# Heads grouped by parity in a fused attention and feed-forward kernel: state products and scores in 64x32 tiles, weight sums continued in one bank, a new order

## The chip, the core and the metric

The kernel runs on one core of a Trainium2 chip. The metric is the device time of one execution in microseconds (us), as the median of several runs. A core has five engines with instruction queues of their own: TensorE (PE, with PEld for its weight loads), VectorE (DVE), ScalarE (ACT), GpSimd (POOL) and SyncE (SP, which here issues most DMAs). Each works through its queue in order and waits on semaphores. TensorE writes to PSUM, eight banks of 512 f32 columns on 128 partitions; the other operands lie in SBUF.

## What is computed

```python
# x [8, 8, 512, 64], state [8, 8, 32, 64]: batch, head, rows, D
scores = scale * x @ state^T                 # softmax over the 32 state rows
xread = softmax(scores) @ state
scores2 = scale * state @ x^T                # softmax over the 512 positions
sread = softmax(scores2) @ x
a = concat([xread, sread], rows)             # 544 rows a batch, heads side by side: 512 features
xn = (a - mean) / sqrt(var + 1e-6) * g_ln
out = a + relu(xn @ w_ch1) @ w_ch2           # w_ch1 [512, 2048], w_ch2 [2048, 512]
```

The weights arrive as 64-bit floats. f32 accuracy is kept by writing each f32 operand as a high and a low f16 half and summing the products high x high, high x low and low x high (`TERMS`).

## The kernel before, in words

*Units.* The 2,048 hidden features are cut into four units of 512 (u = 0 to 3). Because xread is a softmax times the state, xread @ w_ch1 is computed as softmax @ (state @ w_ch1): `state_products` (L660) makes for each batch and unit a `matrix` of 2 x 128 rows (8 heads x 32 state rows) by 512 features, and the products with the softmax numerators `ea` follow in `first_products` (L701, batch 0) and `products` (L799, batches 1 to 7). The second layer is a plain product in batch 0 (L715) and a Strassen form with seven products in batches 1 to 7 and for the 256 state rows at the end (L855, L808). It needs sums and differences of blocks of w2, made once a unit in `sums_of_weights` (L741): products with plus and minus the identity (`signs`), 256 columns each, into parts of two accumulator banks, 16 a unit and half, each difference then split into halves by ACT and DVE.

*Heads.* Heads are paired as g = h // 4, j = h % 4. The state halves `sh` are laid out twice over, so that `sT` [128, g, a, 128] holds, for each head, 64 rows and 64 rows once more; the other operand holds the high half of a head in one half of its 128 partitions and the low half in the other. One product over all 128 rows then gives two of the terms. In the state products (L665) and the scores (L403) a head is a tile of 128 rows x 32 columns; j picks the columns, g the call: eight products of 512 columns (two a, four j) a call. For this, w1's halves are first written to the buffers `raw` or `sums` and then copied by four DMAs a unit into `w1c` (L621), high beside low. The end needs w1's high halves whole, which eight more copies gather in `high` (L891).

*State read.* `read_state` (L475) multiplies, for each head and each of four chunks, the stacked halves of x (128 columns) with both halves of the transposed numerators (64 columns): 32 products (L479). The two 64-row parts of the result are then added by four f32 products with `fold`, two stacked identities (L492), recorded as eight passes.

*PSUM.* `accumulator` is a pool of four banks, `half` of two, `banks` one buffer of two banks. In batches 1 to 7, `banks` is claimed for the maxima, the scores, the state read and twice for mixing (L515); the state products use `half`, which the hidden blocks (L799) also use.

*Order.* The work is written as 175 streams of steps. `PLAN` (L40) lists all steps in one order, as stream:steps, and `issue` (L189) issues them so. Since each engine works in order, this list is each engine's order. Stream 0 is the gain, 1 the attention of batch 0, 2 to 5 the first-layer weights of units 0 to 3, 6 the state products of batch 0, 7 `first_products`, 8 to 11 the second-layer weights, 13 to 16 the second products of batch 0, 17 and 18 attention and state products of batch 1, 19 to 22 the weight sums. All DVE, ACT and POOL work is recorded under L186, the helper that issues a step.

*Weights of a unit* (`weights1`, L581): two loads, 64-bit words to f32 (ACT, DVE), means by four f32 products (L599), four DVE subtractions, sizes (ACT, L608), scale, high half (ACT) and low half (DVE).

Of the kernel before, what the change touches and what calls it, by code (L numbers as in the profile page):

```python
# [1 line left out]

# [6 lines left out]
F32 = mybir.dt.float32  # L9
# [179 lines left out]
def issue(tc, streams, plan):  # L189

    streams = [list(s) for s in streams]
    with tc.manual_schedule():
        for item in plan.split() or [f"{k}:0-{len(s)}" for k, s in enumerate(streams)]:
            k, n = item.split(":")
            n = [int(v) for v in n.split("-")]
            for f in streams[int(k)][n[0]:n[-1] + 1]:
                f()


@with_exitstack  # L200
def moe_attention(ctx: ExitStack, tc: tile.TileContext, x, state, g_ln, w1, w2, out):

    nc = tc.nc
# [24 lines left out]
    def rows(name):  # L233
        return block(8, "rows", 2, name)
# [744 lines left out]
```

## Time and profile before

| | |
|---|---|
| median of 3 runs | 667.59 us (666.89 to 668.29) |
| span of the profiled execution | 665.9 us |
| PE, DVE, ACT, POOL busy | 626.3, 498.0, 388.2, 216.7 us |
| chain that ended last | PE 90%, DVE 5%, DMA 2% |

The profiled execution is told by its span, from the first instruction to the last; the median of the runs is the device's time of whole executions, 1.7 us more. In the profile a group is line, engine, operation, output <- inputs, shape and count. "128*32" is a tile of 128 rows and 32 columns of TensorE. [...] "Chain" is the work followed back from the last instruction, at each step to what released it.

### The profile page before, as it was taken

What the parts mean: (1) busy time and instruction counts of PE and PEld (TensorE: products, weight loads), DVE (VectorE), ACT (ScalarE), POOL (GpSimd) and SP (SyncE); (2) the same over time, 40 slices, a digit from 0 to 9 for tenths busy, and PEclk for the clock granted to TensorE, in tenths of its full rate; (3) what the DMA queues carried; (4) which work ended last, traced back from release to release, by engine and by line L of the source; (5) the groups of instructions that cost most, each with busy time, mean ns of one, the idle gap of its engine ahead of it and who ended that gap; (6) DMA issues with size and microseconds to landing.
All of it is one profiled execution on the core that took longest, in us unless ns stands there. A gap on an engine that the chain in (4) does not pass through costs nothing.

```text
span 665.9 us, 14680 instructions
## 1 busy us (share of the span) xinstructions
PE 626.3 (94%) x5948; PEld 493.1 (74%) x5948; DVE 498.0 (75%) x1002; ACT 388.2 (58%) x699; POOL 216.7 (33%) x189
## 2 busy tenths in 40 slices
PE   0676999999999999999999999999999999999996
PEld 0242755548887887788888888878778887888885
DVE  5989986697788677966887689777976897465533
ACT  5488989667546474547465756465546564344331
POOL 0000333321344325323452226433433343234222
PEclk9977999999999999999999999999999999999998
DMA  8999836924231534330516142305142311244221
GB/s 324 309 278 210 259 103 146 141 57 103 71 74 37 136 104 78 95 94 8 92 32 162 67 88 68 97 5 122 35 126 47 76 32 43 81 116 104 73 56 32
DMA packets 98563, 69.63 MB, mean 105 GB/s; under 512 B 72704, under 2 KB 90624, under 8 KB 98048
## 3 DMA queue, kind: packets, MB, share of 16 engines
q1 hardware_dynamic: 96384, 64.77, 37.5%
q0 software_dynamic: 864, 3.15, 2.6%
q8 instruction: 46, 0.75, 0.5%
q10 hardware_dynamic: 1248, 0.79, 0.4%
q14 instruction: 21, 0.17, 0.1%
HBM read 28.05 MB, written 9.44 MB: 56 GB/s over the span
## 4 chain that ended last, share of the span: by engine, by line
PE 90%; DVE 5%; DMA 2%; ACT 1%; issue 1%; DVEq 0%; SPq 0%
PE acc L855 41%; PE half L799 22%; PE acc L715 6%; PE half L665 5%; PE acc L701 3%; PE half L808 3%; PE acc L747 2%; PE acc L599 2%; PE banks L403 1%; DVE w_t L186 1%; PE banks L479 1%; PE banks L515 1%; PE banks L492 1%; DMA x_f<-in_x_dram 1%; PE acc L608 1%; DMA w1c<-raw 1%
## 5 line engine op out<-in xcount | busy, mean ns | idle before, releaser
L855 PEld LDWEIGHTS <-xs 128*128 128x128 f16 x2520 | 242.4, 98 | 43.6 <-issue 15.3
L186 POOL TENSOR_TENSOR xs<-rs,xs 128x512 f16<-128x512 f32 x120 | 142.4, 1199 | 272.7 <-ACT xs L186 207.1
L855 PE MATMUL acc<-w2h,xs 128*128 128x256 f16 x1440 | 183.0, 273 | 0.0
L799 PE MATMUL half<-ea,matrix 128*128 128x256 f16 x1344 | 159.4, 273 | 0.0
L799 PEld LDWEIGHTS <-matrix 128*128 128x128 f16 x1344 | 130.7, 98 | 16.6 <-issue 0.8
L855 PE MATMUL acc<-sums,xs 128*128 128x256 f16 x1080 | 141.9, 273 | 0.0
L186 DVE SCALAR_TENSOR_TENSOR rs<-half,rs 128x256 f32<-128x256 f32 x224 | 89.4, 419 | 27.6 <-ACT rs L186 13.3
L186 ACT ACTIVATE xs<-rs 128x512 f16<-128x512 f32 x128 | 77.1, 618 | 40.5 <-DVE rs L186 33.8
L186 ACT ACTIVATE xs<-half 128x256 f16<-128x256 f32 (+1 forms) x112 | 53.6, 487 | 72.5 <-PE half L799 50.5
L186 DVE SCALAR_TENSOR_TENSOR xs<-half,xs 128x256 f16<-128x256 f32 (+1 forms) x112 | 61.2, 550 | 28.1 <-ACT xs L186 24.5
L186 ACT ACTIVATE matrix<-half,hs 128x512 f16<-128x512 f32 x56 | 38.0, 687 | 35.2 <-PE half L665 34.9
L186 DVE SCALAR_TENSOR_TENSOR matrix<-half,hs,matrix 128x512 f16<-128x512 f32 x56 | 41.2, 742 | 16.0 <-ACT matrix L186 15.3
L186 ACT ACTIVATE rs<-half 128x256 f32<-128x256 f32 x56 | 21.3, 381 | 42.5 <-PE half L799 40.1
L715 PE MATMUL acc<-w2h,hid 128*128 128x512 f16 x192 | 43.1, 379 | 0.0
L186 DVE TENSOR_TENSOR strip<-acc,strip 128x256 f32<-128x256 f32 (+1 forms) x60 | 33.2, 554 | 10.5 <-PE acc L855 7.5
L665 PE MATMUL half<-w1c,sT 128*32 128x512 f16 x448 | 33.5, 384 | 1.9 <-DVE rs L186 1.0
L186 POOL TENSOR_TENSOR ts<-ts,mA 128x1024 f32<-128x1024 f32 (+1 forms) x8 | 14.4, 1804 | 60.9 <-DVE mA L186 54.5
L715 PEld LDWEIGHTS <-hid 128*128 128x128 f16 x192 | 18.5, 98 | 20.9 <-issue 0.4
L186 DVE SCALAR_TENSOR_TENSOR x<-x_f,x_s,x 128x512 f16<-128x512 f32 x32 | 24.8, 798 | 5.3 <-ACT x L186 5.3
L186 DVE BATCH_NORM_STATS2 s<-xr 128x6 f32<-128x512 f32 x32 | 21.6, 684 | 8.7 <-ACT xr L186 8.6
L186 ACT ACTIVATE x<-x_f,x_s 128x512 f16<-128x512 f32 x32 | 21.7, 713 | 9.8 <-DVE x_s L186 9.8
L186 POOL TENSOR_TENSOR hid<-strip,hid 128x512 f16<-128x512 f32 x16 | 18.5, 1170 | 26.6 <-ACT hid L186 26.5
(152 smaller groups left out, 770.1 us busy)
## 6 DMA issues: line engine op xcount, KB each, us to landing
raw<-in_moe_w_ch_dram SPq DMA_DIRECT2D x9, 1024.0 KB, 7.3
out_dram<-xr SPq DMA_DIRECT2D x16, 512.0 KB, 3.0
x_f<-in_x_dram SPq DMA_DIRECT2D x15, 512.0 KB, 5.6
sums<-in_moe_w_ch_dram SPq DMA_DIRECT2D x7, 1024.0 KB, 8.2
ek<-ea SPq DMA_DIRECT2D x56, 64.0 KB, 2.1
ek<-ek SPq DMA_DIRECT2D x7, 512.0 KB, 4.3
xr<-part POOLq DMA_DIRECT2D x6, 512.0 KB, 5.0
w1c<-raw SPq DMA_DIRECT2D x8, 256.0 KB, 5.1
```

The lines of the kernel that those rows point to most:

```text
L186: return lambda: f(*map(now, args), **{k: now(v) for k, v in kw.items()})
L403: nc.tensor.matmul(o[32 * j:32 * j + 32], lhsT=sT[:, g, a, 32 * j:32 * j + 32], rhs=xT[:, s, 4 * g + j].rearrange("p c t -> p (c t)"), sta ...
L479: nc.tensor.matmul(ps_z[:, h // 4, :, h % 4], lhsT=xv[:, c // hc, h, c % hc], rhs=ebT[:, :, h // 4, c, 32 * (h % 4):32 * (h % 4) + 32], st ...
L492: nc.tensor.matmul(pr[:, g], lhsT=z4[:, g, i], rhs=fold, start=i == 0, stop=i == 1, skip_group_check=True)
L599: nc.tensor.matmul(ps, lhsT=gm[:, k:k + 1].broadcast_to([P, P]), rhs=t4[:, k], start=k == 0, stop=k == 3)
L665: nc.tensor.matmul(ps[32 * j:32 * j + 32], lhsT=sT[:, g, a, 32 * j:32 * j + 32], rhs=w[:, 2 * g + j // 2, j % 2], start=a == 0, stop=a == ...
L701: nc.tensor.matmul(o[:, 256 * f:256 * f + 256], lhsT=m[:, g, i, P * (q + f):P * (q + f) + P], rhs=ea[:, s, k, g], start=f == 0 and g == 0 ...
L715: nc.tensor.matmul(po, lhsT=hid[:, i, q, c * P:(c + 1) * P], rhs=w[:, j, q], start=first and q == 0 and n == 0, stop=last and q == 3 and n ...
L747: nc.tensor.matmul(o, lhsT=signs[:, k // 2], rhs=v[k], start=start and k == 0, stop=k == 3, skip_group_check=True)
L799: nc.tensor.matmul(ps[:, 256 * q:256 * q + 256], lhsT=m[:, h, i, P * (2 * k + q):P * (2 * k + q) + P], rhs=ea[:, 0, j, h, 256 * g:256 * g ...
L808: nc.tensor.matmul(ps[:, 256 * q:256 * q + 256].rearrange("p (t n) -> p t n", t=2), lhsT=w[:, k // 2, k % 2, fs] if k < H else wn[:, k - H ...
L855: nc.tensor.matmul(po[o], lhsT=y[:, n, i, o] if o < 2 else x[:, o - 2, n, i], rhs=v[j], start=u == 0 and n == 0 and k == 0 and o in (2, 1, ...
```

## The change

- Heads are grouped by parity: j = h // 2, g = h % 2. Feature rows 0 to 63 of a chunk of 128 are then head 2j, rows 64 to 127 head 2j + 1, as they lie in w1. x, the state and the results are laid out so.
- `weights1` writes w1's halves straight into `w1c`; the copies go, as do `high` and its copies.
- State products and scores: one call with three terms x four j x two g = 24 products of 512 columns (256 in batch 0's scores), each a tile of 64 rows (g) x 32 columns (j). The two g write to different banks.
- In batches 1 to 7 a unit's state products take `banks` and leave it in one ACT and one DVE pass of 2 x 512 columns.
- State read: three terms in 48 products of 64 columns; ACT and DVE copy a quarter of the result each, and one f32 transpose against the identity takes the place of the fold.
- Weight sums: 12 products of 512 columns a unit; the second and third sum go on in the bank of the first.
- The state rows at the end: 3 x 4 products for each of two parts of a block instead of 12, the same number.
- Batch 0: x is loaded in four pieces by halves of the rows, the states in four; g_ln's load follows them on ACT's queue.
- `PLAN` is new throughout (2,500 steps instead of 2,638).

```diff
 PLAN = (
-    "1:0 1:3-4 1:1-2 1:5-12 4:1 1:19 1:72 0:0 4:6 1:20 1:24-25 4:5 4:7 4:0 4:3 1:17-18 4:2 4:4 3:1 3:6 1:22-23 "
...
+    "0:0 1:2 1:4 1:3 1:1 1:0 1:5-6 4:1 1:7-11 1:71 4:0 1:16 1:12 1:17 1:23-24 1:18 4:6 1:19 4:5 4:2-3 0:1 4:4 2:0 "
...
-        def scores(s, g, o, sT, xT):
-            for a in range(2):
+        def scores(s, ps, sT, xT):
+            for n, (a, i) in enumerate(TERMS):
                 for j in range(4):
...
+                    for g in range(G):
+                        k = hc * (4 * s + j)
+                        nc.tensor.matmul(ps[32 * j:32 * j + 32, g, w * s:w * s + w],
+                                         lhsT=sT[D * g:D * g + D, a, 32 * j:32 * j + 32],
+                                         rhs=xT[D * g:D * g + D, k:k + hc, i], start=n == 0, stop=n == 2,
+                                         skip_group_check=True)
...
+            for j in range(4):
                 for c in range(C):
...
+                    a = hc * (4 * (c // hc) + j) + c % hc
+                    for n, (i, k) in enumerate(TERMS):
+                        nc.tensor.matmul(ps_z[:, j], lhsT=x16[:, a, i], rhs=ebT[:, k, :, c, 32 * j:32 * j + 32],
+                                         start=c == 0 and n == 0, stop=c == C - 1 and n == 2, skip_group_check=True)
...
-        yield do(fold_halves, pr, z4)
...
+        for g, copy in enumerate((partial(nc.scalar.activation, func=AF.Copy), nc.vector.tensor_copy)):
+            r = slice(D * g, D * g + D)
+            yield do(copy, z[r].rearrange("p (j n) -> p j n", j=4), ps_z[r, :, g])
+        yield do(nc.tensor.transpose, pr, z, idf)
...
-        for i in range(2):
-            for s in range(2):
-                to = 64 * (i ^ s)
-                yield do(nc.sync.dma_start, out=w[to:to + 64, :, s], in_=hl[64 * s:64 * s + 64, i])
+        w = narrow(u, "w1c").bitcast(F16).rearrange("p (i e) -> p i e", i=2)
+        yield from split(w[:, 0], w[:, 1], t, scale)
+        w1c[u] = w.rearrange("p i (j f) -> p i j f", j=4)
...
-        def multiply(ps, g, sT, w):
-            for a in range(2):
+        def multiply(ps0, ps1, sT, w):
+            for n, (a, i) in enumerate(TERMS):
                 for j in range(4):
...
+                    for g in range(G):
+                        nc.tensor.matmul((ps0, ps1)[g][32 * j:32 * j + 32],
+                                         lhsT=sT[D * g:D * g + D, a, 32 * j:32 * j + 32],
+                                         rhs=w[D * g:D * g + D, i, j], start=n == 0, stop=n == 2, skip_group_check=True)
...
+            if b == 0:
+                ps = [accumulator() for _ in range(G)]
+                todo = [(ps[g], m[:, g, 0], m[:, g, 1]) for g in range(G)]
+            else:
+                two = banks()
+                ps = [two[:, g] for g in range(G)]
+                todo = [(two, m[:, :, 0], m[:, :, 1])]
+            yield do(multiply, *ps, sT, w1c[u])
...
+        yield do(difference, ps, *b22, *b12)
+        yield do(nc.scalar.activation, t3[0], ps, AF.Copy)
+        yield do(nc.vector.tensor_tensor, t3[1], ps, t3[0], ALU.subtract)
+        yield do(difference, pb, *b12, *b11)
+        yield do(add, 0, False, True, ps, *b11)
...
+        yield do(add, 1, False, True, ps, *b21)
...
```

More of the change, by code (lines that the diff above doesn't have):

```diff
@@ L1 @@
 from contextlib import ExitStack
+from functools import partial
 import concourse.bass as bass
@@ L281, in load_batch @@
         engines = nc.sync, nc.sync if b > 0 else nc.scalar
-        xf = rows("x_f").rearrange("p (h c d) -> p h c d", h=H, c=C)
+        parts = 2 if b == 0 else 1
+        xf = rows("x_f").rearrange("p (s h c d) -> p s h c d", s=parts, h=H, c=C // parts)
         sj = fixed([P, G, D], F32, "s_j")
@@ L285, in load_batch @@
         tiles[:] = xf, sj, sr
-        src = x[b].rearrange("h (p c) d -> p h c d", c=C)
+        src = x[b].rearrange("(j g) (p c) d -> p g j c d", g=G, c=C)
         for hh in range(2):
-            hs = slice(hh * (H // 2), (hh + 1) * (H // 2))
-            yield do(engines[hh].dma_start, out=xf[:, hs], in_=src[:, hs])
-        yield do(nc.sync.dma_start, out=sj, in_=state[b].rearrange("(g j) n d -> (j n) g d", g=G))
+            for g in range(G) if b == 0 else (hh,):
+                o, i = xf[:, hh if b == 0 else 0, 4 * g:4 * g + 4], src[:, g]
+                yield do(engines[hh].dma_start, out=o, in_=i[:, :, 2 * hh:2 * hh + 2] if b == 0 else i)
+        for j in range(4):
+            yield do(engines[j // 2].dma_start, out=sj[32 * j:32 * j + 32], in_=state[b, 2 * j:2 * j + 2].rearrange("g n d -> n g d"))
         for r in range(4 if b > 0 else 0):
@@ L296, in moe_attention @@
     gx = main.tile([P, C], F32, name="gx")
-    nc.scalar.dma_start(out=gx, in_=g_ln.rearrange("(k p) -> p k", p=P))
     idf = main.tile([P, P], F32, name="idf")
     make_identity(nc, idf)
-    fold = main.tile([P, D], F32, name="fold")
-    nc.vector.tensor_tensor(fold, idf[:, 0:D], idf[:, D:2 * D], ALU.add)
     mhalf = main.tile([P, C], F32, name="mhalf")
@@ L336, in gain @@
     def gain():
+        yield do(nc.scalar.dma_start, out=gx, in_=g_ln.rearrange("(k p) -> p k", p=P))
         yield do(nc.vector.tensor_scalar, gm, gx, 1.0 / DM, None, ALU.mult)
-    sh = main.tile([P, G, 2, 2, D], F16, name="sh")
+    sh = main.tile([P, 2, G, D], F16, name="sh")
     sk = main.tile([P, H, D], F16, name="sk")
@@ L355, in attention @@
         am, part = column("x_am", 2), column("x_part", 4)
-        x16 = rows("x16").bitcast(F16).rearrange("p (a i d) -> p a i d", i=2, d=D)
+        x16 = rows("x16").bitcast(F16)
         for q in range(4):
-            v = xf.rearrange("p h c d -> p (h c) d")[:, 8 * q:8 * q + 8]
+            v = xf.rearrange("p s h c d -> p (s h c d)")[:, 512 * q:512 * q + 512]
             if b > 0 or q % 2 == 0:
-                yield do(nc.scalar.activation, x16[:, 8 * q:8 * q + 8].bitcast(BF16)[:, :, 0], v, AF.Abs,
+                yield do(nc.scalar.activation, x16[:, 512 * q:512 * q + 512].bitcast(BF16), v, AF.Abs,
                          accum_out=part[:, q:q + 1])
             else:
-                yield absmax(part[:, q:q + 1], v.rearrange("p a d -> p (a d)"))
+                yield absmax(part[:, q:q + 1], v)
+        x16 = x16.rearrange("p (a i g d) -> p a i g d", i=2, g=G, d=D)
         yield absmax(am[:, 1:2], sj.rearrange("p g d -> p (g d)"))
@@ L371, in attention @@
         yield do(nc.vector.tensor_scalar, es, isx, isst, QK, ALU.mult, ALU.mult)
-        sT = fixed([P, G, 2, P], F16, f"sT_{b % 2}")
-        yield do(nc.scalar.activation, sh[:, :, 0], sj.unsqueeze(2).broadcast_to([P, G, 2, D]), AF.Copy, scale=sst)
-        for i in range(2):
-            yield do(nc.vector.scalar_tensor_tensor, sh[:, :, 1, i], sj, sst, sh[:, :, 0, i], ALU.mult, ALU.subtract)
-        yield do(nc.sync.dma_start_transpose, out=sT.rearrange("p g a n -> p (g a) n"),
-                 in_=sh.rearrange("p g a i d -> p (g a i d)"))
-        xT = (rows("xT") if b > 0 else unit(3, "xT")).bitcast(F16).rearrange("p (s h c t) -> p s h c t", s=parts, h=H, c=hc)
-        xTa = xT.rearrange("p s h c t -> p (s h c) t")
+        sT = fixed([P, 2, P], F16, f"sT_{b % 2}")
+        yield do(nc.scalar.activation, sh[:, 0], sj, AF.Copy, scale=sst)
+        yield do(nc.vector.scalar_tensor_tensor, sh[:, 1], sj, sst, sh[:, 0], ALU.mult, ALU.subtract)
+        yield do(nc.sync.dma_start_transpose, out=sT, in_=sh.rearrange("p i g d -> p (i g d)"))
+        xT = (rows("xT") if b > 0 else unit(3, "xT")).bitcast(F16).rearrange("p (a i t) -> p a i t", i=2, t=P)
+        xTa = xT.rearrange("p a i t -> p (a i) t")
         for q in range(4):
-            s, k = q * parts // 4, q % (4 // parts)
-            nh = H * parts // 4
-            v = xf[:, nh * k:nh * k + nh, hc * s:hc * s + hc]
-            hi, lo = (x16[:, 8 * q:8 * q + 8, i].rearrange("p (h c) d -> p h c d", c=hc) for i in range(2))
+            k, g = divmod(q, 2)
+            v = xf[:, k, 4 * g:4 * g + 4] if parts == 2 else xf[:, 0, 4 * g + 2 * k:4 * g + 2 * k + 2]
+            v = v.rearrange("p h c d -> p (h c) d")
+            hi, lo = (x16[:, 8 * k:8 * k + 8, i, g] for i in range(2))
             yield do(nc.scalar.activation, hi, v, AF.Copy, scale=sx)
@@ L391, in attention @@
                 yield do(nc.sync.dma_start_transpose, out=xTa[:, 8 * q - 8:8 * q + 8],
-                         in_=x16[:, 8 * q - 8:8 * q + 8].rearrange("p a i d -> p (a i d)"))
+                         in_=x16[:, 4 * q - 4:4 * q + 4].rearrange("p a i g d -> p (a i g d)"))
         if b > 0:
@@ L421, in softmax_first @@
         def softmax_first(s):
-            for g in range(G):
-                o = ps[:, g] if parts == 1 else ps[:, s, w * g:w * g + w]
-                yield do(scores, s, g, o, sT, xT)
-            yield do(nc.vector.transpose, cols(ts, s), ps.rearrange("p g t -> p (g t)") if parts == 1 else ps[:, s])
+            yield do(scores, s, ps, sT, xT)
+            o, i = cols(ts, s), ps[:, :, w * s:w * s + w]
+            if parts == 1:
+                yield do(nc.vector.transpose, o, i.rearrange("p g t -> p (g t)"))
+            else:
+                for g in range(G):
+                    yield do(nc.vector.transpose, o[:, w * g:w * g + w], i[:, g])
         def softmax_rest(s):
@@ L461, in attention @@
         rB = column("rB", G)
[L462 removed]
+        eBf = eB.rearrange("p g t -> p (g t)")
         yield do(nc.scalar.activation, eb[:, 0], eBf, AF.Copy, scale=SE)
@@ L612, in weights1 @@
         yield from scales(m, scale, is1[:, u:u + 1])
-        hl = raws[1].bitcast(F16).rearrange("p (i e) -> p i e", i=2)
-        yield from split(hl[:, 0], hl[:, 1], t, scale)
-        hl = hl.rearrange("p i (k f) -> p i k f", k=4)
-        w = narrow(u, "w1c").bitcast(F16).rearrange("p (k s f) -> p k s f", k=4, s=2)
-        w1c[u] = w
-        for i in range(2):
-            for s in range(2):
-                to = 64 * (i ^ s)
-                yield do(nc.sync.dma_start, out=w[to:to + 64, :, s], in_=hl[64 * s:64 * s + 64, i])
+        w = narrow(u, "w1c").bitcast(F16).rearrange("p (i e) -> p i e", i=2)
+        yield from split(w[:, 0], w[:, 1], t, scale)
+        w1c[u] = w.rearrange("p i (j f) -> p i j f", j=4)
     def weights2(u):
@@ L743, in sums_of_weights, with add @@
         w = w2h[u].rearrange("p i (k n) e -> p i n k e", n=2)
-        def subtract(start, o, *v):
-            for k in range(4):
-                nc.tensor.matmul(o, lhsT=signs[:, k // 2], rhs=v[k], start=start and k == 0, stop=k == 3,
+        def add(sign, first, last, ps, *v):
+            for i in range(2):
+                nc.tensor.matmul(ps, lhsT=signs[:, sign], rhs=v[i], start=first and i == 0, stop=last and i == 1,
                                  skip_group_check=True)
-        for n in range(2):
-            ps = [accumulator() for _ in range(2)]
-            (b21, b22), (b11, b12) = ([[w[:, i, n, k, 256 * x:256 * x + 256] for i in range(2)] for x in range(2)]
-                                      for k in range(2))
-            t3, t2, n4 = ([sums16[:, u, k, i, n] for i in range(2)] for k in range(3))
-            o = [v[:, 256 * x:256 * x + 256] for v in ps for x in range(2)]
-            for pairs in (((t3, b22, b12), (b12, b12, b11)), ((t2, b22, b12),), ((n4, b21, t2),)):
-                first = len(o)
-                def subtract_all(*v, first=first):
-                    for k in range(len(v) // 5):
-                        subtract(first != 1 and k == 0, *v[5 * k:5 * k + 5])
-                todo = [(d, a, b, o.pop(0)) for d, a, b in pairs]
-                yield do(subtract_all, *[v for d, a, b, p in todo for v in (p, *a, *b)])
-                for d, a, b, p in todo:
-                    yield do(nc.scalar.activation, d[0], p, AF.Copy)
-                    yield do(nc.vector.tensor_tensor, d[1], p, d[0], ALU.subtract)
@@ new lines, in difference @@
+        def difference(ps, a0, a1, b0, b1):
+            add(0, True, False, ps, a0, a1)
+            add(1, False, True, ps, b0, b1)
+        (b21, b22), (b11, b12) = ([[w[:, i, :, k, 256 * x:256 * x + 256] for i in range(2)] for x in range(2)]
+                                  for k in range(2))
+        t3, t2, n4 = ([sums16[:, u, k, i] for i in range(2)] for k in range(3))
+        ps, pb = (accumulator().rearrange("p (n e) -> p n e", n=2) for _ in range(2))
+        yield do(difference, ps, *b22, *b12)
@@ L818, in block @@
                         else:
-                            yield do(first_of_state, ps, k, w1c[u], high[u], state_rows_T[0])
+                            yield do(first_of_state, ps, k, w1c[u], state_rows_T[0])
                             r = rs[:, 512 * k:512 * k + 512]
@@ L887, in products @@
             yield together()
-    high, state_rows_T = [None] * U, [None]
-    def high_halves(u):
-        high[u] = quad("high").bitcast(F16).rearrange("p (k f) -> p k f", k=4)
-        for s in range(2):
-            half = slice(64 * s, 64 * s + 64)
-            yield do(nc.sync.dma_start, out=high[u][half], in_=w1c[u][half, :, s])
+    state_rows_T = [None]
     def state_rows():
@@ L937, in moe_attention @@
         streams += these
-    streams += [list(state_rows()), *(list(high_halves(u)) for u in range(U))]
+    streams += [list(state_rows())]
     streams += [list(s) for s in products(B)]
```

95 lines of the change are left out of this document (39 added, 56 removed), and 243 rows, old and new, of the table PLAN.

## The prediction

> **What bounds the kernel now.** I read the page first, then the busy times of three stretches, then the waits in the first stretch and the chain in the second.
>
> ```profile
> span 665.9 us, 14680 instructions
> ...
> PE 626.3 (94%) x5948; PEld 493.1 (74%) x5948; DVE 498.0 (75%) x1002; ACT 388.2 (58%) x699; POOL 216.7 (33%) x189
> ...
> PE   0676999999999999999999999999999999999996
> ...
> DVE  5989986697788677966887689777976897465533
> ```
>
> ```profile
> 0.00:64.00 64.00, 33.66 (x205) 15.62 (x205) 52.85 (x95) 41.95 (x56) 2.79 (x8) 0.87 0.94 284
> 64.00:660.10 596.10, 592.66 (x5745) 477.44 (x5744) 443.07 (x905) 346.27 (x644) 213.92 (x181) 1.00 0.35 85
> 660.10:665.90 5.80, 0.00 (x0) 0.00 (x0) 2.11 (x3) 0.00 (x0) 0.00 (x0) 0.70 0.33 90
> ```
>
> The columns are length, then PE, PEld, DVE, ACT, POOL, granted clock, DMA share and GB/s. There are two regimes. Until 64 us PE idles for 30.3 of 64.0 us while DVE works 52.85: the start is set by turning weights into halves. From 64 to 660.1 us PE lacks 3.4 us of 596.1, at clock 1.00. So every microsecond taken from PE's own list after 64 us is a microsecond of the span, and no other engine's saving is, unless it makes PE wait. DVE, the next, has 443 us in that stretch: 153 us of room.
>
> ```profile
> by line: PE acc L855 45.4%; PE half L799 24.0%; PE acc L715 7.0%; PE half L665 5.0%; PE acc L701 3.9%; PE half L808 3.5%; PE acc L747 2.4%; PE banks L479 1.2%; PE banks L403 1.2%; PE banks L515 1.1%; PE banks L492 1.0%; PE banks L186 0.5%;
> ```
>
> This is the chain of 64 to 660 us by line. L855, L799, L715, L701, L515 and L808 keep their number and shape of products (L808 sums 24 a block by another split). The change edits L665 (state products), L403 (scores), L479 (state read), L492 (fold) and L747 (weight sums): 10.8% of 596 us, some 64 us.
>
> **The change part by part.** The chain, in order of time, gives each unit price (start, length, what):
>
> ```profile
> 127.76 0.98 PE banks L403 x16
> 128.73 1.42 PE acc L701 x12
> ...
> 148.57 1.31 PE acc L747 x12
> 149.88 0.55 PE half L665 x8
> 150.43 1.42 PE half L799 x12
> 151.85 1.75 PE acc L747 x16
> 153.59 1.31 PE half L799 x12
> ...
> 157.52 0.93 PE banks L479 x32
> 158.46 1.31 PE half L799 x12
> 159.76 0.84 PE banks L492 x8
> ```
>
> A product of 256 columns costs 1.31 / 12 = 0.109 us, so one of 512 costs 0.216. Eight products of 128x32 tiles cost 0.55, sixteen 0.98: four tiles run at once, a round of 512 columns is (0.98 - 0.55) / 2 = 0.215 us, and 0.12 is entry. The twelve products after such a set cost 1.42 instead of 1.31: 0.11 more for going back to 128x128. A set therefore is 0.23 + 0.215 a round.
>
> *State products, batches 1 to 7.* Before: two sets of eight a unit, 56 in all. The chain gives them 5.0% of 596.1 = 29.8 us, and 0.11 after some 51 separate sets is 5.6: 35.4 us. After: one set of 24 products a unit, in 64x32 tiles. If all eight tiles run at once, that is three rounds: 0.23 + 3 x 0.215 + 0.03 for eight starts = 0.90 us, 28 times: 25.2. Gain 10.2 us. No row shows a tile of 64 rows. The nearest row for row parts is the mixing of batch 0 (L530, 32-row tiles):
>
> ```profile
> L530 PE MATMUL acc<-sh,ea x96: 185/188/237, 42.3 to 76.1; 32*128 32x64 f16 x96
> ...
> 48.24 0.52 PE L530 MATMUL acc<-sh,ea 32*128 32x64 f16 x12
> ...
> 43.69:43.70 0.01, 0.01 (x6) 0.01 (x3) 1.00 0.99 410
> 43.80:43.81 0.01, 0.01 (x11) 0.01 (x6) 1.00 0.99 410
> ```
>
> The first row gives minimum, median and maximum duration: 188 ns. Twelve products of one row quarter take 0.52 us, so they start (0.52 - 0.19) / 11 = 0.03 us apart, and one stream has at most seven under way at a time. The last rows count what is under way in 10 ns (PE, then PEld). At 43.80 us it is eleven: two row quarters, writing the same 128 PSUM partitions in different banks, run at once. The new code gives its two row halves different banks too, so I take full overlap. Bounds: 0.90 us a set, and 3.0 where the halves exclude each other (a rival below).
>
> *Scores, batches 1 to 7.* The same step: 1.2% of 596.1 = 7.2 us plus about nine returns (1.0) becomes 7 x 0.90 = 6.3: gain 1.9.
>
> *State read.* 32 products of 64 columns in 0.93 us are 0.029 each. 48 such cost 1.39: a loss of 0.46 x 7 = 3.3 us. It buys the next item.
>
> *Fold.* Eight passes, 0.84 us, become one transpose of 128 columns. The nearest row is the transpose of the maxima:
>
> ```profile
> 172.51 0.27 PE L186 MATMUL banks<-idf,x_am 128*2 128x128 f32 x1
> 172.51 0.21 PEld L855 LDWEIGHTS <-xs 128*128 128x128 f16 x2
> 172.62 0.27 PE L855 MATMUL acc<-sums,xs 128*128 128x256 f16 x1
> ```
>
> The next product starts 0.11 us later. It loads two columns, the new one 128, so 0.11 to 0.22; I take 0.11: gain 0.73 x 7 = 5.1 us (4.3 at the other end).
>
> *Weight sums.* 4 units x 2 x 4 x 4 = 128 products of 256 columns (14.0 us) become 4 x 12 = 48 of 512 (10.4): gain 3.6. Each addition into the bank waits until ACT and DVE have read it; before, each later difference waited for the halves of the earlier one too, and PE lost nothing by it after 64 us. I price that wait at 0.
>
> Sum on PE's list: -10.2 - 1.9 + 3.3 - 5.1 - 3.6 = -17.5 us.
>
> *Evacuation.* The state products leave `half` (two buffers) for `banks` (one of two banks), in one pass of 1,024 per engine.
>
> ```profile
> L186 DVE SCALAR_TENSOR_TENSOR matrix<-half,hs,matrix 128x512 f16<-128x512 f32 x56 | 41.2, 742 | 16.0 <-ACT matrix L186 15.3
> L186 ACT ACTIVATE xr<-banks,ux 128x1024 f32<-128x1024 f32 x14 | 15.6, 1111 | 6.0 <-PE banks L515 5.3 <-DMA s_r<-in_state_dram 0.5
> L186 DVE SCALAR_TENSOR_TENSOR ea<-ef,ea 128x1024 f16<-128x1024 f32 x7 | 9.3, 1332 | 0.7 <-ACT ea L186 0.4
> ```
>
> ACT takes about 1.11 us; DVE between 1.33 (that row) and 1.48 (twice 742): some 2.6 us in which `banks` is held. What is queued behind a claim of `banks` is all of PE. In the new PLAN I counted PE's products between each of these 28 sets and the next claim: at least 2.6 us, mostly over 3. So 0, with up to 0.9 us in the few tight places (a rival).
>
> *The start.* The 16 copies of w1c go; the halves are written in place.
>
> ```profile
> 0.74 5.62 DMA x_f<-in_x_dram
> ...
> 16.35 9.30 PE acc L599 x16
> ...
> 52.55 5.25 DMA w1c<-raw
> ...
> 65.43 2.67 PE acc L701 x12
> ...
> 83.98 2.59 PE acc L715 x12
> ```
>
> ```profile
> 49.53 4.61 DVE L186 SCALAR_TENSOR_TENSOR raw<-w_t,of_weights,raw 128x2048 f16<-128x2048 f32 x2
> 54.06 2.72 DVE L186 SCALAR_TENSOR_TENSOR w_t<-w_t,gx,acc 128x512 f32<-128x512 f32 x4
> ...
> PE acc L665 <- DMA w1c<-raw: 3.7, 1, 3.7
> ```
>
> PE waited 3.7 us for a copy. The larger effect is the order: in the old PLAN the first L701 step (7:0) stands behind the low halves of w1 units 0, 1 and 2 and the four subtractions of unit 3. In the new one it stands behind the low half of unit 0 alone: two low halves (4.61) and four subtractions (2.72), 7.3 us of DVE work, come after it. DVE being 83% busy there, L701 can start 7 to 11 us sooner. Late next is the first L715, which needs w2's halves, hence DVE work that is not removed, only some of it moved. I take 6 us, between 0 (all given back at L715) and 11 (7.3 + 3.7). Costs at the start: x of batch 0 comes in pieces of 512 B instead of 1,024, same bytes, 0 to 2 us on the 5.62 that head the chain, taken as 0 within the 6; two more issues on ACT's queue lie under that load, for which ACT waits; g_ln's load, now behind them, has until the first means (L599) at 16.35. The batch-0 edits on PE fall into its 30.3 idle us: 0. On SP 24 issues go (w1c, high) and three a batch for s_j come, far ahead of their use: 0. Fewer columns in the last transpose and no `high` copies: PE does not wait there now: 0.
>
> Total -23.5 us. The span goes from 665.9 to 642.4. The median of the runs, 667.6, stands 1.7 us above the profiled span; carried over, the forecast is 644.1.
>
> **The rivals.**
>
> *The row halves exclude each other (slower).* The new loop issues both halves of a column tile one after the other, in order. If the second had to wait, the next tile could start only with it: 13 steps of 0.215 and 0.23, 3.0 us a set, 2.1 more in 35 sets: +74, 718 us. It beats the gain from 23.5 / 35 = 0.67 us a set, a set of 1.57 us. Against it stand the eleven L530 products. 4%.
>
> *The rounds do not overlap (no change).* If each round's loads waited for the round before, a round would cost a product and a load.
>
> ```profile
> L665 PEld LDWEIGHTS <-sT x6: 92/92/96, 149.8 to 149.8; 128*32 128x32 f16 x6
> L665 PE MATMUL half<-w1c,sT x4: 389/390/390, 149.8 to 149.8; 128*32 128x512 f16 x4
> ```
>
> 0.39 + 0.09 = 0.48, three rounds and the return 1.55 us, 0.65 more in 35 sets: +23, 667 us. The rows, cut at 149.83 us, speak against it: six loads are out while the four first products, on all rows, are under way. [...] 3%.
>
> *`banks` becomes the wait (slower).* Were each of the 28 sets followed too closely, PE would wait up to 2.6 us each time, 73 us, 717; from 23.5 / 28 = 0.84 us each it is slower than before. For it: nine claims a batch on one buffer, where there were five. Against it: the counted distances. 4%.
>
> *The start gives nothing back.* L715 waits for w2 as late as before: 650 us, still faster. 25%.
>
> **How the numbers follow.** My case has 64%, the poor start 25%, no change 3%, slower 8%. 0.2% (1.3 us) is about what a measurement of this kernel can tell. The predicted time is 644. Low end: the start gives all 11 us (639) and the new order closes the 3.4 us of waits and some more of the idle start: 634. High end: the poor start (650) plus 14 tight claims at half a microsecond: 657. Faster 0.89, same 0.03, slower 0.08.
>
> **What would show it.** State product sets of 24 at about 0.8 us start to end, followed at 0.11 by the next form; the two row halves starting within 10 ns. L479's successor at 48 products in 1.4 us, one transpose near 0.1, 48 sums of 0.216. PE after the start again without idle, no PE wait on `banks`. First L701 near 56 to 58 us, and PE's idle time before the saturated stretch some 24 us. Sets above 1.5 us, or PE idle of more than 10 us after the start, would make the prediction wrong.

## The result

| | before | after |
|---|---|---|
| median of the runs | 667.94 us (666.89 to 668.80, 4 runs) | 651.54 us (649.83 to 652.74, 4 runs) |
| span of the profiled execution | 665.9 us | 650.0 us |

The ratio is 0.9759 with a 95% interval of 0.9738 to 0.9780: 16.4 us faster, where 23.5 were forecast. The median lies within the range given, 7.5 us above the value given. In the profiled executions the difference is 15.9 us; the accounts below are made against that.

The page of the changed kernel:

```profile
span 650.0 us, 15182 instructions
...
PE 610.9 (94%) x6268; PEld 482.5 (74%) x6268; DVE 482.1 (74%) x958; ACT 372.0 (57%) x655; POOL 215.1 (33%) x189
...
PE   0858999999999999999999999999999999999995
...
DVE  4899888887587678786787688768876887456523
```

and its busy times in the same three stretches (length, PE, PEld, DVE, ACT, POOL, clock, DMA share, GB/s):

```profile
0.00:64.00 64.00, 36.38 (x251) 17.42 (x252) 51.95 (x92) 40.79 (x52) 3.96 (x10) 0.87 0.78 259
64.00:643.30 579.30, 574.55 (x6024) 465.04 (x6020) 428.05 (x865) 331.25 (x604) 211.11 (x180) 1.00 0.33 79
643.30:650.00 6.70, 0.00 (x0) 0.00 (x0) 2.10 (x3) 0.00 (x0) 0.00 (x0) 0.79 0.29 80
```

The two regimes are still there. PE lost 15.4 us of busy time and its idle time is nearly what it was: 27.6 us before 64 us (30.3 before the change), 4.8 in the long stretch (3.4), and 6.7 at the end (5.8). PE's list became shorter; the start was not shortened with it.

The chain of the changed kernel around its new pieces (start, length, what):

```profile
114.05 0.86 PE acc L746 x4
114.91 0.77 PE banks L407 x24
115.68 0.97 PE acc L746 x4
...
120.55 0.77 PE banks L657 x24
121.32 0.54 PE acc L746 x2
...
129.64 1.40 PE banks L481 x48
...
139.82 0.11 PE banks L192
```

A set of 24 in 64x32 tiles takes 0.77 us, the four sums behind a set 0.97 where four behind a full-size product take 0.86 (0.11 for the return), 48 products of the state read 1.40, the transpose in the fold's place 0.11. Each price is within 0.04 us of the one in the prediction.

The whole difference, in four parts, by start-to-start times of PE's products in the two traces (in the L747 set of before at 148.57 us a product of 256 columns lasts 0.27 us and the next starts 0.11 us after it; the second is its price):

| part | forecast | measured |
|---|---|---|
| PE's own list, batches 1 to 7 | -17.5 | -17.6 |
| the start, to 100 us | -6 | -0.6 |
| PE's waits after it | 0 | +1.4 |
| from PE's last product to the end | 0 | +0.9 |
| sum | -23.5 | -15.9 |

The list is: state products 34.4 to 24.1 (-10.3; before, 2.0 us of waiting stand beside them), scores 7.9 to 6.3 (-1.6), state read 6.6 to 9.8 (+3.2), fold 6.1 to 0.8 (-5.3), weight sums 14.0 to 10.4 (-3.6). The waits are 3.4 us after the change and 2.0 before it (by the profile's own list of waits 2.8 and 1.9). The start is counted by what PE had done at 100 us: 11 more second products of batch 0 (61 against 50, 2.4 us), but two units of state products fewer (1.7 us).

### The profile page after: what moved, and what is told of

Its sections match the earlier page's. It is cut to its first block, busy times and chain, and to the rows that moved or that the text cites. A ratio compares the mean times of both kernels' runs of the same rounds, so it can differ in the third digit from the quotient of the medians.

```text
span 650.0 us, 15182 instructions
## 1 busy us (share of the span) xinstructions
PE 610.9 (94%) x6268; PEld 482.5 (74%) x6268; DVE 482.1 (74%) x958; ACT 372.0 (57%) x655; POOL 215.1 (33%) x189
## 4 chain that ended last, share of the span: by engine, by line
PE 80%; DVE 9%; ACT 6%; DMA 2%; issue 1%; ACTq 0%; SPq 0%; DVEq 0%
PE acc L859 39%; PE half L801 21%; PE acc L714 4%; PE half L811 3%; PE banks L657 3%; DVE w_t L192 2%; PE acc L700 2%; PE acc L746 2%; PE banks L481 1%; DMA xT<-x 1%; PE acc L596 1%; PE banks L512 1%; ACT x L192 1%; DVE rs L192 1%; ACT strip L192 1%
## 5 line engine op out<-in xcount | busy, mean ns | idle before, releaser
L859 PEld LDWEIGHTS <-xs 128*128 128x128 f16 x2520 | 243.2, 98 | 38.4 <-issue 8.9
L192 POOL TENSOR_TENSOR xs<-rs,xs 128x512 f16<-128x512 f32 x120 | 140.6, 1183 | 274.3 <-ACT xs L192 203.4
L859 PE MATMUL acc<-w2h,xs 128*128 128x256 f16 x1440 | 182.3, 273 | 0.0
L801 PE MATMUL half<-ea,matrix 128*128 128x256 f16 x1344 | 161.5, 273 | 1.3 <-DVE xs L192 1.3
L801 PEld LDWEIGHTS <-matrix 128*128 128x128 f16 x1344 | 130.3, 98 | 19.9 <-issue 2.3
L859 PE MATMUL acc<-sums,xs 128*128 128x256 f16 x1080 | 141.7, 273 | 0.0
L192 ACT ACTIVATE xs<-rs 128x512 f16<-128x512 f32 x128 | 76.9, 619 | 57.1 <-DVE rs L192 48.9
L192 ACT ACTIVATE xs<-half 128x256 f16<-128x256 f32 (+1 forms) x112 | 53.1, 485 | 75.4 <-PE half L801 34.4
L192 DVE SCALAR_TENSOR_TENSOR matrix<-banks,hs,matrix 128x1024 f16<-128x1024 f32 x28 | 35.7, 1274 | 13.9 <-ACT matrix L192 13.9
L714 PE MATMUL acc<-w2h,hid 128*128 128x512 f16 x192 | 43.6, 379 | 0.6 <-DVE w2h L192 0.4
L192 ACT ACTIVATE matrix<-banks,hs 128x1024 f16<-128x1024 f32 x28 | 31.1, 1110 | 12.8 <-PE banks L657 12.8
L714 PEld LDWEIGHTS <-hid 128*128 128x128 f16 x192 | 18.5, 98 | 22.5 <-issue 1.1
L596 PE MATMUL acc<-w_t,gm 128*128 128x512 f32 x32 | 19.5, 761 | 12.3 <-DVE w_t L192 7.7
L192 ACT ACTIVATE x<-x_f,x_s 128x512 f16<-128x512 f32 x32 | 21.9, 715 | 10.4 <-DVE x_s L192 10.4
```

Source lines behind the costliest of these rows:

```text
L192: return lambda: f(*map(now, args), **{k: now(v) for k, v in kw.items()})
L596: nc.tensor.matmul(ps, lhsT=gm[:, k:k + 1].broadcast_to([P, P]), rhs=t4[:, k], start=k == 0, stop=k == 3)
L714: nc.tensor.matmul(po, lhsT=hid[:, i, q, c * P:(c + 1) * P], rhs=w[:, j, q], start=first and q == 0 and n == 0, stop=last and q == 3 and n ...
L801: nc.tensor.matmul(ps[:, 256 * q:256 * q + 256], lhsT=m[:, h, i, P * (2 * k + q):P * (2 * k + q) + P], rhs=ea[:, 0, j, h, 256 * g:256 * g ...
L859: nc.tensor.matmul(po[o], lhsT=y[:, n, i, o] if o < 2 else x[:, o - 2, n, i], rhs=v[j], start=u == 0 and n == 0 and k == 0 and o in (2, 1, ...
```

## The experiments

Theory 1: after the start PE's list is the time, and the start gave nothing because another chain, DVE's list, ended as late as the one that was taken away. Its rivals: the gain is the new order's; the start hangs on ACT; DVE's list had set the start all along, so that there had been nothing to take. The changed kernel itself was timed again beside three of the runs below (the row halves, the sums, DVE's first step). The others ran on three other chips, on which the kernel before had medians of 667.4 to 668.0 us, for 667.6 here; differences of half a microsecond between them say nothing.

> The changed kernel once more, unaltered, as the yardstick for the others on this chip: 651.5 us (650 to 653) against 667.9 of the kernel before. Nothing is told apart by it.

651.37 us (650.62 to 652.74): the yardstick of what follows.

### The row halves one after the other

```diff
-            for n, (a, i) in enumerate(TERMS):
-                for j in range(4):
-                    for g in range(G):
+            for g in range(G):
+                for n, (a, i) in enumerate(TERMS):
+                    for j in range(4):
                         nc.tensor.matmul((ps0, ps1)[g][32 * j:32 * j + 32],
```

> The two row halves of the state products one after the other instead of side by side (the loop over g outermost): three rounds of eight tiles become six rounds of four, of which the third and fourth can still overlap, so five. Theory A (each microsecond of PE's own list after the start is a microsecond of the time, and the 0.86 us of a set come from the eight tiles running at once): a set goes from 0.86 to 0.86 + 2 x 0.215 = 1.29 us, 28 sets, +12.0 us: 663.5; the four sets of batch 0 lie in PE's idle time. Theory B (the gain came from the new order and fewer waits, the sets lie beside other work): less than +4 us, at most 655. Theory C (the halves already ran one after the other): 651.5.

651.06 us (650.57 to 651.74): no change. All three theories missed why. A piece of its chain, and what is under way in two windows of 10 ns of that set (PE, then PEld; one product in each count belongs to the work ahead):

```profile
118.64 0.80 PE banks L657 x24
```

```profile
118.59:118.60 0.01, 0.01 (x5) 0.01 (x8) 0.01 (x1) 0.01 (x2) 0.00 (x0) 1.00 0.00 0
118.63:118.64 0.01, 0.01 (x9) 0.01 (x16) 0.01 (x1) 0.01 (x2) 0.00 (x0) 1.00 0.00 0
```

Four products of the set run at 118.59 and eight at 118.63. Counted from the first, the trace has the starts at 0 to 10 ns (4), 40 to 50 (4), 227 to 237 (4), 267 to 277 (4), 443 to 453 (4) and 483 to 493 (4). It does not name the row half of a product, but the starts tell it: the rounds of the changed kernel, on the same tiles, start 216 to 226 ns apart, so the four at 40 to 50 ns can't be the first half's second round. They are of the second half, although eight products of the first half stand between them in the program: the second half did not stand behind the waiting rounds of the first. That an engine works through its queue in order, as was said at the start, does not hold for PE in this set. The set still has three rounds, and 0.80 us for 0.77. So this edit did not lengthen a set and could not test the list.

### One round twice

```diff
-            for n, (a, i) in enumerate(TERMS):
+            terms = TERMS[:1] * (b > 0) + TERMS
+            for n, (a, i) in enumerate(terms):
...
-                                         rhs=w[D * g:D * g + D, i, j], start=n == 0, stop=n == 2, skip_group_check=True)
+                                         rhs=w[D * g:D * g + D, i, j], start=n <= len(terms) - 3, stop=n == len(terms) - 1,
+                                         skip_group_check=True)
```

> The first round of eight products of each state-product set of batches 1 to 7 is issued twice (the second start overwrites the first, so the values stay). Putting the row halves one after the other had cost nothing (a set of 0.80 us instead of 0.77), so that edit could not tell whether a longer set costs time; this one lengthens each of 28 sets by one round of 0.215 us. Theory A (after the start PE's own list sets the time): +6.0 us, 657.4 against 651.4. Theory B (the sets lie beside other work, the gain came from the order): under +1 us, at most 652.4.

654.80 us (654.59 to 656.82), +3.4: between the two. In its chain a set is

```profile
118.41 0.99 PE banks L658 x32
```

0.99 instead of 0.77, and the sets together take 30.9 us after 84 us instead of 24.9: +6.0, as A has it. From the first second product to PE's last product it is +5.3 us (565.6 against 560.3). The rest was won ahead of that: its first second product comes at 80.6 us instead of 82.8, with the clock at half for 17.1 us instead of 20.5, in a stretch that the edit does not touch. So the list theory holds where it speaks, after the start. Why the start came sooner was not tested; in the run of the row halves, too, the first second product came at 80.9 us, with the clock at half for 10.2 us. B, under 1 us, is out. In this trace all line numbers behind the edit are one or two higher.

### The sums alone

The kernel before with the 48 sums of 512 columns:

```diff
-        for n in range(2):
-            ps = [accumulator() for _ in range(2)]
...
+        ps, pb = (accumulator().rearrange("p (n e) -> p n e", n=2) for _ in range(2))
+        yield do(both, ps, pb, *b22, *b12, *b11)
...
+        yield do(add, 0, False, True, ps, *b11)
```

> The kernel before with one part of the change alone: the weight sums as 48 products of 512 columns, continued in one bank, all at the places where the second column half stood. Theory A (PE's list sets the time there, and the waits for ACT and DVE between the additions are hidden): -3.6 us, 664.3 against 667.9. Theory B (each addition waits for ACT and DVE to read the bank, about 1.2 us eight times, and the products behind wait with it): 667.9 or more.

678.31 us (677.70 to 680.40), 10.7 us slower than the kernel before beside it. It settles nothing: at the places of the old order the next addition comes, in some units, before the first sum has been read, so other sums are computed, and PE waits behind them (3.0 us once for DVE's half of a sum). It does show that the form needs an order of its own; the -3.6 us of this term rest on the trace of the changed kernel alone.

### DVE's first step

```diff
-    "0:0 1:2 1:4 1:3 1:1 1:0 1:5-6 4:1 1:7-11 1:71 4:0 1:16 1:12 1:17 1:23-24 1:18 4:6 1:19 4:5 4:2-3 0:1 4:4 2:0 "
+    "0:0 1:2 1:3 1:1 1:4 1:0 1:5-6 4:1 1:7-11 1:71 4:0 1:16 1:12 1:17 1:23-24 1:18 4:6 1:19 4:5 4:2-3 0:1 4:4 2:0 "
```

In the changed kernel the chain begins with the load of the states, for which DVE waits with the maxima of x queued behind:

```profile
2.44 5.22 DMA s_j<-in_state_dram
```

> One edit of the order: DVE takes the two maxima of x ahead of the maximum of the state, which lands last (7.66 us). Theory A (from 7.8 to 56.7 us the chain is DVE's list, so the start begins when DVE begins): the scale x_s comes 1.2 us sooner, the first L700 at about 56.3 instead of 57.5, and the time falls by 1.0 to 1.3 us, to 650.3. Theory B (the landing of w1 or ACT's list sets the start, DVE only looks full): x_s comes 1.2 us sooner and nothing else does; 651.5 within 0.5.

650.59 us (649.79 to 651.53), 0.8 less in the median. By median alone the intervals overlap (0.9732 to 0.9764, and 0.9745 to 0.9779 for the unaltered kernel); the profile is clear. First L700, first L714 and PE's last product all come 1.0 to 1.1 us sooner (56.3 for 57.4, 81.8 for 82.8, 642.0 for 643.1): what DVE gains at 8 us is kept to the end. Theory A.

### Less for DVE, after the change and before it

Both runs leave out the three lowest bits of the weights' mantissas:

```diff
-            yield do(nc.vector.tensor_scalar, low, low, 29, None, ALU.logical_shift_right)
-            yield do(nc.vector.scalar_tensor_tensor, t[:, 1024 * fh:1024 * fh + 1024].bitcast(U32), high.bitcast(U32),
-                     3, low, ALU.logical_shift_left, ALU.bitwise_or)
+            yield lambda: None
+            yield do(nc.vector.tensor_scalar, t[:, 1024 * fh:1024 * fh + 1024].bitcast(U32), high.bitcast(U32), 3, None,
+                     ALU.logical_shift_left)
```

> Leaves out the three lowest mantissa bits of the weights: DVE's shift of the low word goes (16 of 0.61 to 0.68 us) and the joining step becomes a plain shift (1.23 us to about 0.7). DVE has some 19 us less to do in the first 100 us, about 9 of them ahead of the first L700. Theory A (until 57 us DVE's list sets the start, and the copies that the change removed were not on it): the first L700 comes at 48 to 52 us, and 3 to 6 us of it are left at the end, the rest being taken by ACT (35.5 of 36.0 us busy from 64 to 100): 645.5 to 648.5. Theory B (ACT's list sets the start all along): under 1 us, 650.5 to 651.5.

In the changed kernel: 646.10 us (645.57 to 646.78), 5.3 less. The first L700 comes at 51.5 us (57.4), the first L714 at 76.7 (82.9). Its stretches, and those of the changed kernel as it is:

```profile
40.00:57.00 17.00, 14.02 (x135) 8.51 (x136) 15.10 (x26) 15.78 (x21) 1.05 (x1) 0.76 0.77 216
57.00:64.00 7.00, 5.77 (x117) 4.32 (x115) 5.45 (x7) 7.00 (x16) 2.27 (x2) 1.00 0.00 0
64.00:100.00 36.00, 34.24 (x251) 19.74 (x259) 26.64 (x63) 35.84 (x53) 11.62 (x11) 1.00 0.59 168
```

```profile
40.00:57.00 17.00, 9.86 (x91) 4.37 (x90) 16.73 (x34) 16.32 (x20) 2.09 (x2) 0.70 0.67 201
57.00:64.00 7.00, 7.00 (x81) 5.42 (x79) 6.79 (x9) 5.82 (x12) 1.17 (x2) 0.78 0.06 14
64.00:100.00 36.00, 33.82 (x287) 20.43 (x284) 31.86 (x64) 35.44 (x56) 12.95 (x12) 0.95 0.42 134
```

With DVE relieved, PE works 14.0 of the 17 us from 40 to 57 instead of 9.9. ACT, 7.0 of 7.0 and 35.8 of 36.0, is then the one with no room left.

> The kernel before with the same relief of DVE as in the run without the shift (the three lowest mantissa bits of the weights are left out, some 19 us less for DVE in the first 100 us). Theory A (the start of the kernel before, too, was set by DVE's list as a whole, and the waits for the copies of w1 lay beside it, so that taking the copies away had nothing to give): the first L715 comes 4 to 7 us sooner than 84.0 and the time falls by 4 to 6 us, as it did after the change (5.3): 662 to 664. Theory B (the copies and PE's own list set that start, and the change put DVE in their place): at most 2 us, 665.9 to 667.9.

The same relief in the kernel before: 669.42 us (666.36 to 670.43) against 667.71, ratio 1.001 with an interval of 0.9994 to 1.0027. Nothing. DVE falls from 84.1 to 67.5 us busy in the first 100, yet the first L715 comes at 86.0 (83.8). One piece of its chain and one row of its waits show what held it:

```profile
50.27 7.36 DMA w1c<-raw
```

```profile
PE acc L665 <- DMA w1c<-raw: 5.8, 1, 5.8
```

Before the change this copy was issued at 52.55 and landed at 57.80. Now it is issued 2.3 us sooner and lands at 57.63: the DMA share is 1.05 from 40 to 57 us (0.85 before), and the copy takes 7.36 us instead of 5.25. The first L715 is later by 2.2 us, and two stretches of L701 that fell into the half clock in this execution took 2.4 us more (4.81 and 5.70 us, for 4.04 and 4.04 before; granted clock from 64 to 100 us 0.91, for 0.95). The fastest of the twelve runs, 666.36, is no better than the fastest of the kernel before, 666.71, either. So the start before did hang on the copies, and not on DVE; B is right in kind. With the copies in place, relieving DVE gives nothing; with the copies gone, it gives 5.3 us: DVE's list was the next bound behind them.

### Less for ACT

```diff
-        yield do(nc.scalar.activation, hi, r, AF.Copy)
+        yield do(engine.tensor_copy, hi, r)
         yield do(engine.tensor_tensor, lo, r, hi, ALU.subtract)
```

> The 16 roundings of the first products' halves (0.63 us each) go from ACT to GpSimd, which works 12.9 of the 36 us from 64 to 100; ACT has 10 us less. Theory A (from 57 to 100 us ACT's list sets the start): the first L714 comes 1 to 3 us sooner than 82.8, PE's 3.9 us of idle time between 57 and 100 us shrink by 2 or more, and the time falls by 2 to 4 us: 647.5 to 649.5. Theory B (DVE, 31.9 of the same 36 us, is as late): within 0.7 of 651.4. Theory C (GpSimd's rounding and difference in a row come later than ACT's did): slower by up to 2 us.

659.56 us (659.03 to 660.24), 8.2 slower: C has the direction, but not the size. GpSimd's groups from 40 to 110 us:

```profile
L192 POOL TENSOR_TENSOR hid<-strip,hid 128x512 f16<-128x512 f32 x11 | 16.4, 1499 | 0.6
L192 POOL CAST hid<-strip 128x512 f16<-128x512 f32 x11 | 14.7, 1334 | 13.1 <-ACT strip L192 13.1
```

The rounding takes 1.33 us there in the mean (0.63 on ACT) and the difference behind it 1.50 instead of 1.21: 2.8 us a block in a row. The means hide the spread. Three of the eleven roundings take 0.61 us, as little as on ACT, and the longest takes 2.67; the differences go from 1.14 to 3.08. The two longest steps lie beside DVE's low halves of w1 (`w1c`), which themselves take 3.24 and 3.04 us there, for 2.34 in the changed kernel: GpSimd and DVE were slow together, and why was not tested.

The chain shows a second cost, which no theory had:

```profile
103.97 1.39 POOL hid L192
105.36 5.10 DMA xr<-part
...
110.54 0.70 ACT part L192
...
111.28 1.48 PE acc L657 x20
```

GpSimd also issues the transfers that add the partial results to `xr`. In the changed kernel two of them are issued one behind the other, from 97.14 us on; here a rounding that waits for ACT stands ahead of the second, which is issued at 105.36 and lands at 110.46. ACT waits 3.3 us for it, and PE behind ACT 2.7. From 100 to 165 us PE, always busy before, idles 3.4 us in all, and the clock is at half again for 6.8 us there: granted 0.95 in the mean. Whether ACT alone is the next bound of the start stays open, since this run moved the work to a place where it held up other work; that it is full is seen above, that its relief would pay is not shown.

### Products that nobody reads

```diff
-WARM = 0
+WARM = 63
```

with their places in `PLAN`: 20 ahead of the first scores, 9 ahead of the second sum of sizes, 3 ahead of the second scores, 20 ahead of the last means, 7 ahead of the first state products, 4 ahead of the first mixing.

> 63 products that nobody reads (0.216 us each at the full clock) are put into PE's idle times of the start, ahead of the scores, the sums of sizes, the last means, the first state products and the first mixing. The granted clock is at half for 20.5 us of the start, and the 24 products of L700 at 57.4 us take 4.0 us instead of 2.6. Theory A (the half clock costs the start what the runs with a mean clock of 0.990 show): the clock stays full from 36 to 60 us, the first L714 comes 1.5 to 2.5 us sooner, 649.0 to 650.0. Theory B (DVE and ACT set the start, the clock lies under them): 651.4 within 0.5. Theory C (the products hold up what DVE waits for): slower by up to 2 us.

653.67 us (653.17 to 654.99), 2.3 slower, with the clock full throughout (mean 0.998). Theory C, and the wait is on the list of DVE's waits from 20 to 60 us:

```profile
DVE ts L204 <- PE banks L419: 3.0, 1, 3.0
```

(L419 of this kernel is L407 of the changed one.) PE was not idle where the first 20 stand: the means of two units (L596, f32) run there until 32.6 us. The scores came 3.8 us later and DVE waited 3.0 for them. DVE being the chain, the first L714 came at 83.9.

### Mending the order

`late` has DVE's first step as above and moves three steps:

```diff
-101:38 94:9 81:90 92:12 101:39 94:13 93:1 94:12
+94:9 81:90 92:12 94:13 93:1 101:38 94:12 101:39
...
-121:41 121:50 116:5 114:8 101:74 113:2 114:10
+121:41 116:5 114:8 101:74 113:2 114:10 121:50
```

> Order alone: DVE's maxima of x first, as before, and two later places mended: the scores of batch 5 (PE waited 0.9 us there for the transposed x, at 386 us) go one step of L859 later, and the row maxima of batch 6's scores (1.21 us of DVE, at 455 us) go behind the two steps that free a half bank, for which L801 waited 1.3 us. Theory A (what PE waits for after the start is added to the time): 1.0 + 0.7 + 1.2 us less than the changed kernel: 648.3 to 649.3. Theory B (the waits only move to the next step): 650.6, as with the first edit alone.

649.82 us (648.48 to 652.04): B's 650.6 and A's upper end 649.3 lie on both sides, and the spread is 3.6 us. PE's waits from 100 us on, of the changed kernel and then of this one:

```profile
PE half L801 <- DVE xs L192: 1.3, 1, 1.3
PE banks L407 <- DMA xT<-x: 0.9, 1, 0.9
PE acc L714 <- ACT strip L192: 0.2, 1, 0.2
PE banks L192 <- ACT z L192: 0.2, 1, 0.2
PE banks L192 <- DVE x_am L192: 0.2, 1, 0.2
```

```profile
PE acc L867 <- POOL xs L200: 0.8, 1, 0.8
PE half L809 <- DVE xs L200: 0.6, 1, 0.6
...
PE banks L415 <- DMA xT<-x: 0.2, 1, 0.2
```

L867, L809 and L415 are L859, L801 and L407 of the changed kernel. The scores' wait went from 0.9 to 0.2. The other only moved: 0.8 and 0.6 for 1.3. No wait of the changed kernel is on `banks` for its evacuation.

`best` adds 31 unread products, in true gaps only (9 ahead of the second sum of sizes, 18 ahead of the last means, 4 ahead of the first mixing).

> The same order, with 31 of the products that nobody reads in the three gaps in which PE stood idle in the trace (34.3, 41.3 and 54.5 us) and none of those that had come ahead of the scores and of the state products, where they held up DVE by 3.0 us. Theory A (the half clock costs the start about 2 us): 1.5 to 2.5 us less than the same order without them, 646.5 to 647.5. Theory B (the clock lies under DVE and ACT): no difference.

648.32 us (648.09 to 648.72), 1.5 less than `late` in the median, clock 0.999. The fastest runs of the two are 0.4 apart, the slowest 3.3: between these two kernels, what the full clock took away is the spread. It does not explain all of the spread, since `warm`, with the clock as full, ran from 653.17 to 654.99. In the starts of the traces the clock is at half in stretches of 3.4, 6.8, 10.2 and 13.7 us, at other places from kernel to kernel (31.0 to 37.8, 44.6 to 48.0, 54.9 to 61.7 and 65.1 to 68.5 us in the kernel before, 36.1 to 49.8, 56.6 to 60.0 and 66.9 to 70.3 us in the changed one, 38.7 to 48.9 alone in that of the row halves). Where one fell on a busy PE it cost time: the 24 products of L700 at 57.4 took 4.0 us in the changed kernel's profile and started 0.21 us apart until 60.0 us (clock 0.50) and 0.11 apart after it (0.99); 24 such products at clock 1.00 took 2.62 us before the change (L701 at 97.26).

`best_tail` takes back the step at 455 us and issues the last stores in the old order:

```diff
-170:12-16 170:7-9 170:11 170:10
+170:12 170:15 170:14 170:16 170:13 170:7 170:10-11 170:9 170:8
```

> The order of the last kernel with the products that nobody reads, less the edit at 455 us (it had only moved PE's wait: 1.0 and 0.8 us at two places for 1.4 at one), and with the last eight stores issued in the order of the kernel before (one queue's store first where the changed kernel has the other's). From PE's last product to the end the changed kernel takes 6.75 us, the kernel before 5.82. Theory A (that order of issues is what the end lost): 6.75 becomes 5.8, and the time 648.3 - 0.9 - 0.4 = 647.0. Theory B (the stores land late for another reason): 647.9 to 648.3.

647.63 us (647.33 to 648.07), ratio to the kernel before 0.9706 (0.9693 to 0.9720): the fastest full computation of this study, 3.7 us below the changed kernel as timed in the first experiment. Against the kernel before, timed beside each, it and `best` are level (0.9706 and 0.9701), so the 0.7 us between their medians is not shown to be a gain. In the traces PE's last product to the end is 6.45 us, for 6.77 in the changed kernel and 5.82 before: part of what A expected. The queues of the changed kernel's last 6.7 us hold one more row than before the change, where only q1 and q10 stand:

```profile
q14 instruction: 1, 0.01, 0.3%
```

One packet of a queue of instructions, the last traffic of that stretch, and `best_tail` has it too. That it is the remaining 0.6 us was not tested.

## Why the prediction was right and wrong

*State products:* -10.2 forecast, -10.3 measured. *Scores, state read, fold, sums:* each within 0.3 us. The unit prices from the chain of before carried over to a tile shape that no row of it showed, with the bound chosen by the nearest row (the mixing of batch 0).

*The start:* this is the step that failed: "I take 6 us, between 0 (all given back at L715) and 11". Its parts were right. The first L700 was put at 56 to 58 and came at 57.4, 8.0 us sooner. PE's idle time before the saturated stretch was put at 24 us and was 27.6. Wrong was the size of what comes next, and the lead can be followed in the counts of products started:

| started by (us) | 57 | 65 | 84 | 100 |
|---|---|---|---|---|
| before: first (L701), second (L715) | 0, 0 | 0, 0 | 108, 1 | 144, 50 |
| after: first (L700), second (L714) | 0, 0 | 36, 0 | 120, 3 | 144, 61 |
| before: mixing of 96, sizes of 16 | 48, 12 | 66, 16 | 96, 16 | 96, 16 |
| after: mixing of 96, sizes of 16 | 7, 12 | 60, 12 | 96, 16 | 96, 16 |

L700 was brought ahead of work that had stood ahead of it, the mixing and the sizes of the last unit, and that work then had to be done. At 84 us the lead is 14 products. The prediction read "PE idles 30.3 us" and "PE waited 3.7 us for a copy" and did not ask how late DVE's list would be without the copy: DVE was 83% busy there, which I took as room and which was nearly the next bound. "The start gives nothing back", 650 us at 25%, is what happened, by the mechanism named for it: the second products come nearly as late as before (82.9 us for 83.8). What stands behind it is in the chain of the changed kernel, here of its second timing:

```profile
48.01 1.23 DVE w_t L192
...
50.09 2.25 DVE w1c L192
...
56.05 0.61 DVE ea L192
...
57.42 4.03 PE acc L700 x24
61.48 0.61 ACT strip L192
...
79.42 0.85 ACT w2h L192
80.27 5.87 DMA sums<-in_moe_w_ch_dram
...
92.13 1.89 ACT w1c L192
...
99.16 0.49 ACT strip L192
...
99.69 2.75 PE acc L714 x12
```

DVE's list heads it from 24 to 57 us, and from 69 to 100 it runs on ACT, with one load of weights between, where the chain before the change was almost wholly on PE from 64 us on. That the median still lies in the range is owed to the range's high end, which started from this rival.

*x of batch 0 and the states in pieces, "taken as 0 within the 6":* the scale x_s comes at 11.5 instead of 10.1 us, not because of x but because DVE waits for the states first (ACT begins on x at 4.90 us, 5.83 before, so the smaller pieces of x show no cost); 1.0 us of it was won back by one exchange.

*Waits, "PE after the start again without idle":* +1.4. Two places of the new order hold most of the 3.4 us: the transposed x of batch 5 (0.9 by the profile's list) and a half bank that DVE frees late because it works on the row maxima of batch 6 (1.3). *`banks` becomes the wait:* none on it. *The rounds do not overlap:* 0.77 us against the 1.44 of that rival; it fell. *The row halves exclude each other:* fell too, and its price was built on products being taken in program order, which the trace of the halves one after the other contradicts (the second half's first four start 40 ns after the first's).

*The end, at no cost:* +0.9, cause open.

## What to carry to other kernels

A list of one saturated engine can be priced product by product from start-to-start times, and here the sum held to 0.1 us and each of its terms to 0.3; a start cannot, because removing its bound gives only the distance to the next one. Before pricing a start, add up the lists of all engines up to the point in question, without the step that goes. And look whether a step that comes sooner is really a lead: count what else had been done by then.

## What the runs showed of the hardware

- In a set of the run of the row halves (118.59 us) TensorE did not start products of different 64x32 tiles in program order: four began 40 ns after the first, ahead of eight that stand before them in the program.
- In the changed kernel eight 64x32 tiles run at once with starts 2 to 5 ns apart; 24 products of 512 columns take 0.77 us, and 32, with one round twice, 0.99: 0.22 for a round.
- With less for ACT, GpSimd rounded 128x512 f32 to f16 in 0.61 us at best and 2.67 at worst (mean 1.33); ScalarE took 0.63 in the changed kernel. The longest steps lie beside DVE's low halves of w1, which went from 2.34 to 3.24 us.
- In the kernel before without the shift, at a DMA share of 1.05, a copy issued 2.3 us sooner landed 0.2 us sooner.
- Executions of one kernel differed by up to 4.1 us (the kernel before without the shift); with PE's gaps filled and a mean clock of 0.995 to 0.999, by 0.6 to 1.8. How much of this is the place of the half clock was not measured.
